# One-token attention with a gate: the queries' matrix in one load, the keys of pair 13 in one load, and the output matrix in eight pieces instead of nine

## The chip, the cores and the metric

The kernel runs on one core of one Trainium2 chip. The metric is the device time of one execution in microseconds (us). The kernel before takes 685.77 us, the median of three runs (685.71 to 686.2). All data is float32.

## The reference

The input is one token `x` of 512 numbers. It is normalised, and then goes two ways: attention of 32 heads over a cache of 8192 keys and values of 128 numbers each, and a gated product (GLU) whose result gates the attention's output.

```python
xn = layernorm(x)                                   # (1, 1, 512)
q = (xn @ wq).reshape(32 heads, 128)                # wq: 512 x 4096
p = softmax(q . k_cache * 128**-0.5)                # k_cache: 32 x 8192 x 128
o = p @ v_cache                                     # v_cache: 32 x 8192 x 128
s = o.reshape(4096) @ wo                            # wo: 4096 x 512
h = sigmoid(xn @ w_gate) * (xn @ w_up)              # 512 x 1376 each
g = silu(h @ w_down)                                # 1376 x 512
out = x + s * g
```

Keys and values are 134.2 MB each, `wq` and `wo` 8.4 MB each, the three matrices of the GLU 2.8 MB each: 293.7 MB that are each read once.

## The kernel before, in words

**Work and tiles.** Two heads make a pair, so there are 16 pairs (0 to 15). One pair's keys, or its values, are 8.4 MB: 128 partitions with 64 KB each (128 rows of 128 numbers; the heads lie on 64 partitions each). SBUF has three such slots. Slots 0 and 1 take keys: pair i lies in slot (i + 1) mod 2. Slot 2 takes values, and before them `wq` (four rows of 4096 per partition, 64 KB) and then `w_down`. Slot 0 first holds `w_gate` and `w_up`, slot 1 at the end `wo` (32 rows of 512 per partition, 64 KB).

**The loads.** All large loads are issued by SyncE (SP) on one queue, in one fixed order: `wq`, `w_gate`, `w_up`, keys 0, `w_down`, keys 1, values 0, keys 2, values 1, keys 3 and so on to values 15, then `wo`. SP waits ahead of an issue until the slot is free: keys i wait for the end of the scores of pair i-2 (`summed[i - 2]`), values i for the end of the products of pair i-1 (`valued`; for the first halves of the last two, `halved`). `w_down` waits until `wq` has been used up (`spread_all`), keys 1 until the GLU's first products are made (`rows[1]`), values 0 until the gate is made (`gated`). A load of 2 KB, `x`, comes in by ScalarE's queue.

**Ahead of the pairs.** VectorE (DVE) makes `xn`. Then `in_place` (lines 285 to 289) works on `wq` in its slot: for k = 0 to 2 it multiplies row k of each partition by its number of `xn` and adds it to row 0; the last row is added in eight parts of 512 (line 306). TensorE (PE) sums each part over the partitions with a matrix of ones, and ScalarE (ACT) copies it to the queries. The same `in_place` follows for `w_gate` and `w_up`.

**One pair.** `scores(i)` on DVE waits for the keys, multiplies them with the query (line 414) and sums them over the 128 numbers (line 415), piece by piece where the load was cut; a maximum goes by PE and DVE (`all_max`), ACT makes the powers (`powers_of`), PE multiplies them with the values (`pair`), and ACT and DVE take the result out (`parts`, `heads_out`). `K_CUTS` says where the keys' loads are cut: those of pairs 13 and 14 at three quarters, those of pair 15 at a half. `V_CUTS` cuts the last values.

**The end.** `wo` comes in pieces of whole rows r (0 to 31) that end at `W_ENDS`, so the first piece has ten rows and the last one row. Each row is 512 numbers on 128 partitions, multiplied with column r of `o_all`. Three ways share them: the rows of `W_DVE` are added up on DVE (lines 506 to 517, in order, two sums by turns); the rows of `W_PE` go through PE to `big[0]`, row number k of the list to group k mod 4 of the output's partitions; rows 28 to 31 (`direct`) go through PE to `acc`. `to_fold` adds DVE's sum and `big[0]` on DVE, `fold` adds that over the partitions into `acc` on PE. In PE's program `fold` stands between rows 30 and 31. Lines 538 and 540 gate the result and add `x`, and SP writes it out.

PE's instructions are noted down first and played later, so in the trace all of them have line 41.

Of the kernel before, what the change touches and what calls it, by code (L numbers as in the profile page):

```python
# [54 lines left out]
def kernel(  # L55
# [18 lines left out]
    NB = S // HP  # L74
    NP = H // 2
# [15 lines left out]
    FC = FL // GP  # L91
    assert F <= 3 * QT and FL % GP == 0 and 2 * KT * F <= SLOT and (FP + FC) * D <= SLOT // 2

    W_ENDS, W_FOLD = (10, 16, 20, 23, 26, 28, 30, 31, 32), 28
    W_PE = [0, 1, 10, 16, 17, 20, 21, *range(24, W_FOLD)]
    W_DVE = [r for r in range(W_FOLD) if r not in W_PE]
    V_CUTS, K_CUTS = (NB // 2, NB * 13 // 16), {NP - 3: (NB * 3 // 4,), NP - 2: (NB * 3 // 4,), NP - 1: (NB // 2,)}

    N_SEMS = 40
    DVE, ACT, SP, POOL = nc.vector, nc.scalar, nc.sync, nc.gpsimd  # L100
    PE = Later(nc.tensor)
    pe_only = OrderedEngineSet([nc.tensor.engine])
# [2 lines left out]

    sems = [nc.alloc_semaphore(f"s_{i}") for i in range(N_SEMS)]
    s_out = tc.alloc_semaphore("s_out")
# [45 lines left out]
    def semaphore(name):  # L153
        return unused.pop(0)
# [14 lines left out]
    def load(eng, name, dst, src, *after):  # L169
        wait(eng, *after)  # L170
        if name not in loads:
            loads[name] = [semaphore(f"s_{name}"), 0]
        loads[name][1] += 16
        eng.dma_start(dst, src).then_inc(loads[name][0], 16)  # L174
        return loads[name][0], loads[name][1]

    def wait(eng, *steps):
        for s in steps:
            if s is not None:
                eng.wait_ge(*s)  # L180
# [10 lines left out]
    xv = x.rearrange("a b d -> (a b d)")  # L191
    wq_t = slots[2].rearrange("p (k c) -> p k c", k=KT)
    wq_v = wq.rearrange("(p k) c -> p k c", k=KT)
    ld_wq = [load(SP, f"wq{n}", wq_t[:, n:n + 2, :], wq_v[:, n:n + 2, :]) for n in (0, 2)]
    wg_t, wu_t = (slots[0][:, n * KT * F:(n + 1) * KT * F].rearrange("p (k f) -> p k f", f=F) for n in range(2))
    ld_g = load(SP, "wg", wg_t, w_gate.rearrange("(p k) f -> p k f", k=KT))
    ld_u = load(SP, "wu", wu_t, w_up.rearrange("(p k) f -> p k f", k=KT))
# [62 lines left out]
    t = dve(DVE.reduce_sum(st[:, 0:1], x_col, axis=AX.X))  # L260
    wait(PE, t)
    t = pe(PE.matmul(pt[:, 0:1], ones, st[:, 0:1], start=True, stop=True))
    wait(DVE, t)
    t = dve(DVE.tensor_scalar(st[:, 1:2], pt[:, 0:1], 1.0 / D, None, op0=ALU.mult))
    wait(DVE, t)
    t = dve(DVE.tensor_scalar(xc, x_col, st[:, 1:2], None, op0=ALU.subtract))
    wait(DVE, t)
    t = dve(DVE.tensor_mul(sq, xc, xc))
    wait(DVE, t)
    t = dve(DVE.reduce_sum(st[:, 2:3], sq, axis=AX.X))  # L270
    wait(PE, t)
    t = pe(PE.matmul(pm[:, 0:1], ones, st[:, 2:3], start=True, stop=True))
    wait(ACT, t)
    t = act(ACT.activation(st[:, 3:4], pm[:, 0:1], AF.Sqrt, bias=eps_t, scale=1.0 / D))
    wait(DVE, t)
    t = dve(DVE.reciprocal(st[:, 4:5], st[:, 3:4]))
# [8 lines left out]
    def in_place(w, k, cols=slice(None)):  # L285
        y = w[:, 0, cols]
        if k == 0:
            return dve(DVE.tensor_scalar(y, y, xn[:, 0:1], None, op0=ALU.mult))
        return dve(DVE.scalar_tensor_tensor(y, w[:, k, cols], xn[:, k:k + 1], y, op0=ALU.mult, op1=ALU.add))  # L289
# [1 line left out]

    wait(DVE, c_xn)
    for k in range(KT - 1):
        wait(DVE, ld_wq[k // 2] if k % 2 == 0 else None, t if k else None)
        t = in_place(wq_t, k)
    wait(DVE, t)
    before_q = PE.take()
# [36 lines left out]
    for dst, src, ld in zip(sums, (wg_t, wu_t), (ld_g, ld_u)):  # L334
        wait(DVE, ld)
        for k in range(KT):
            t = in_place(src, k)
# [7 lines left out]
    for d, c in zip(sums[0], chunks):  # L345
        t = act(ACT.activation(sg[:, c], d[:, :c.stop - c.start], AF.Sigmoid))
    wait(DVE, t, rows[1])
    for d, c in zip(sums[1], chunks):
        t = dve(DVE.tensor_mul(hg[:, c], sg[:, c], d[:, :c.stop - c.start]))
# [6 lines left out]
    n = FL // NG  # L356
    for g in range(NG):
        r = slice(g * GP, (g + 1) * GP)
        h = hg[r, NG * FW + g * n:NG * FW + (g + 1) * n].rearrange("p (i c) -> p c i", c=FC)
        t = dve(DVE.transpose(hid[r, FP:, :].rearrange("p c (i m) -> p c i m", m=NG),  # L360
                              h.unsqueeze(3).to_broadcast([GP, FC, n // FC, NG])))
# [125 lines left out]
    def to_fold(after):  # L487
        wait(DVE, after, t_part)
        return dve(DVE.tensor_add(s_tmp, part[0], big[0]))
# [11 lines left out]
    def landed(eng, r, rows):  # L501
        k = rows.index(r)
        wait(eng, piece[r] if k == 0 or piece[r] != piece[rows[k - 1]] else None)

    t_parts = [placed, None]
    for k, r in enumerate(W_DVE):
        n = k % 2
# [11 lines left out]
    wait(PE, placed)  # L519
    for k, r in enumerate(W_PE):  # L520
        g = k % NG * GP
        landed(PE, r, W_PE)
        ins = PE.matmul(big[0][g:g + 1, :], o_all[:, r:r + 1], wo_t[:, r, :],
                        start=(k < NG), stop=(k + NG >= len(W_PE)))
    folded = to_fold(pe(ins))
# [12 lines left out]
    t = dve(DVE.tensor_mul(g_row, g_row, acc))  # L538
    wait(DVE, t)
    t = dve(DVE.tensor_add(g_row, g_row, x_row))  # L540
# [64 lines left out]
```

## Time and profile before

| | |
|---|---|
| three timed runs | 685.71, 685.77, 686.2 us |
| the profiled execution | 686.37 us |
| its span, from the first to the last instruction | 684.5 us |
| busy: VectorE, TensorE, ScalarE | 615.2, 218.1, 44.6 us |
| moved by the loads' queue | 293.67 MB at 429 GB/s over the span |

The profiled execution's time is 1.9 us over its span, and 0.6 us over the median of the timed runs. The trace lists for each engine its instructions with start and length in us from the start of the span, and how long the engine stood idle before one and for what. A row of the timeline may hold several like instructions (x4). SPq is SyncE's queue of issues, PEld is TensorE's loading of weights. The view by stretches gives, for chosen stretches of time, each engine's busy time and its count of instructions, the TensorE clock that was granted (1.00 is full speed), and last the loads: the time of those packets that began in the stretch as a share of it, and their bytes per second.

### The profile page before, as it was taken

The page shows a single profiled execution, that of the slowest core. Times are in us where ns is not written, and L with a number is a line of the kernel's source. Part 1 is how long each engine was busy: PE and PEld are TensorE (multiplying, and loading weights), DVE is VectorE, ACT ScalarE, POOL GpSimd, SP SyncE. Part 2 cuts the span into 40 slices and gives each one's busy share as a digit, 9 for nine tenths or more (in the row PEclk, how much of TensorE's full clock was granted, in tenths as well). Part 3 has the DMA queues.
Part 4 walks back from the last instruction along what each step waited for, and adds up shares of the span by engine and source line. Part 5 has one row for each costly group of instructions (what it writes and reads, how often), then busy time and mean ns, then how long its engine had stood idle before and what let it go on. Part 6 is the DMA issues. An engine that isn't in the chain of part 4 may idle for free. (4 is left out here: it accounts for less than half of the span.)

```text
span 684.5 us, 3423 instructions
## 1 busy us (share of the span) xinstructions
PE 218.1 (32%) x1376; PEld 61.9 (9%) x1376; DVE 615.2 (90%) x156; ACT 44.6 (7%) x142; POOL 2.6 (0%) x11
## 2 busy tenths in 40 slices
PE   0353024060513306050512406050512406060666
PEld 0120001010100101010100101010100101010110
DVE  3879999999999898998989898998989999999917
ACT  2130010000000100000000100000010101000010
POOL 0000000000000000000000000000000000000000
PEclk9996657575665757575665757575665757575886
DMA  9999999999999999999999999999999999999997
GB/s 372 433 444 463 437 429 429 429 429 429 429 429 429 429 429 429 437 463 448 429 429 429 429 429 429 429 429 429 444 467 393 472 414 414 460 419 438 429 418 320
DMA packets 7554, 293.71 MB, mean 429 GB/s; under 512 B 856, under 2 KB 864, under 8 KB 1664
## 3 DMA queue, kind: packets, MB, share of 16 engines
q1 hardware_dynamic: 7544, 293.67, 99.4%
q8 instruction: 2, 0.03, 0.0%
q10 hardware_dynamic: 8, 0.00, 0.0%
HBM read 293.67 MB, written 0.00 MB: 429 GB/s over the span
## 5 line engine op out<-in xcount | busy, mean ns | idle before, releaser
L414 DVE TENSOR_TENSOR slot<-slot,q_all 128x16384 f32<-128x16384 f32 (+3 forms) x19 | 275.9, 14522 | 21.8 <-DMA slot<-in_A_k_cache_dram 21.8
L415 DVE TENSOR_REDUCE sc<-slot 128x128 f32<-128x16384 f32 (+3 forms) x19 | 276.0, 14525 | 0.7
L41 PE MATMUL psum<-slot,zeros 128*8 128x512 f32 x1024 | 147.2, 734 | 262.9 <-PEq L41 262.9
L41 PEld LDWEIGHTS psum<-slot,zeros 128*8 128x8 f32 x1024 | 30.3, 103 | 366.3 <-issue 366.3
L41 PE MATMUL psum<-ident,mx 128*1 128x128 f32 x32 | 8.7, 371 | 105.6 <-PEq L41 105.6
L436 ACT COPY o<-psum 128x512 f32<-128x512 f32 x16 | 9.4, 586 | 408.2 <-PE psum L41 408.2
L41 PE MATMUL psum<-slot,ones 128*128 (+3 forms) x36 | 15.9, 612 | 22.9 <-PEq L41 17.5
L289 DVE SCALAR_TENSOR_TENSOR slot<-slot,xn 128x1376 f32<-128x1376 f32 (+1 forms) x8 | 18.9, 2360 | 3.0 <-DMA slot<-in_A_wq_dram 2.7
L41 PE MATMUL psum<-o,pick 128*2 128x128 f32 x128 | 16.5, 272 | 12.8 <-PEq L41 12.8
L422 DVE STREAM_TRANSPOSE psum<-psum 32x128 f32<-32x128 f32 x16 | 5.0, 310 | 11.1 <-PE psum L41 11.1
L429 ACT ACTIVATE zeros<-sc,nb 64x128 f32<-64x128 f32 x32 | 12.8, 399 | 0.9
L41 PEld LDWEIGHTS psum<-o,pick 128*2 128x2 f32 x128 | 9.9, 84 | 29.6 <-issue 27.2
L41 PE MATMUL psum<-slot,o_all 128*1 128x128 f32 (+1 forms) x54 | 10.8, 514 | 5.2 <-DMA slot<-in_A_wo_dram 5.2
L427 ACT ACTIVATE nb<-psum 128x2 f32<-128x2 f32 x16 | 2.8, 172 | 147.9 <-PE psum L41 147.9
L41 PEld LDWEIGHTS psum<-ident,mx 128*1 128x1 f32 x32 | 1.9, 80 | 109.6 <-issue 109.5
L407 DVE TENSOR_REDUCE mx<-psum 1x2 f32<-1x128 f32 x16 | 4.4, 277 | 7.8 <-PE psum L41 7.8
L41 PE MATMUL psum<-zeros,rs 128*32 128x2 f32 x32 | 3.8, 187 | 23.5 <-PEq L41 23.5
L41 PE MATMUL psum<-mx,ones 1*128 1x2 f32 x32 | 8.4, 331 | 7.4 <-PEq L41 7.4
L514 DVE SCALAR_TENSOR_TENSOR q_all<-slot,o_all,q_all 128x512 f32<-128x512 f32 x15 | 10.0, 747 | 0.0
L41 PE MATMUL psum<-slot,o 128*1 128x512 f32 x26 | 5.7, 944 | 13.0 <-DMA slot<-in_B_w_down_dram 13.0
L41 PEld LDWEIGHTS psum<-slot,ones 128*128 128x128 f32 (+1 forms) x36 | 6.3, 197 | 32.2 <-issue 24.5
L41 PEld LDWEIGHTS psum<-mx,ones 1*128 1x128 f32 x32 | 7.5, 290 | 14.3 <-issue 14.3
(54 smaller groups left out, 60.4 us busy)
## 6 DMA issues: line engine op xcount, KB each, us to landing
slot<-in_A_k_cache_dram SPq DMA_DIRECT2D x2, 6144.0 KB, 37.9
slot<-in_A_v_cache_dram SPq DMA_DIRECT2D x3, 4096.0 KB, 22.6
slot<-in_A_wq_dram SPq DMA_DIRECT2D x2, 4096.0 KB, 16.8
slot<-in_A_k_cache_dram SPq DMA_DIRECT2D x2, 4096.0 KB, 40.5
slot<-in_A_k_cache_dram SPq DMA_DIRECT2D x2, 2048.0 KB, 42.4
slot<-in_B_w_gate_dram SPq DMA_DIRECT2D x1, 2752.0 KB, 27.5
slot<-in_B_w_up_dram SPq DMA_DIRECT2D x1, 2752.0 KB, 33.5
slot<-in_B_w_down_dram SPq DMA_DIRECT2D x1, 2560.0 KB, 23.8
```

The costliest lines, as they stand in the source:

```text
L41: ins = getattr(self.engine, name)(*args, **kwargs)
L289: return dve(DVE.scalar_tensor_tensor(y, w[:, k, cols], xn[:, k:k + 1], y, op0=ALU.mult, op1=ALU.add))
L407: DVE.reduce_max(mx[:1, 1:3], pt[0:1, :].rearrange("o (e p) -> o e p", e=2), axis=AX.X).then_inc(reduced, 1)
L414: wait(DVE, dve(DVE.tensor_mul(k[:, j, :], k[:, j, :], qb[:, i:i + 1, :].to_broadcast([P, n, Dh]))))
L415: summed[i] = dve(DVE.reduce_sum(sc[i % 2][:, j], k[:, j, :], axis=AX.X))
L422: turned_out[i] = dve(DVE.transpose(o, pn.rearrange("e (a r) -> e a r", r=WR)))
L427: wait(ACT, act(ACT.mul(nb, pm[:, :2], -SCALE)))
L429: ACT.activation(weights[h, :, e * HT:(e + 1) * HT], sc[i % 2][h].rearrange("p (g b) -> p g b", b=HT), AF.Exp, bias=nb[h, e:e + 1], scale= ...
L436: ACT.copy(o1, po).then_inc(copied, 1)
L514: ins = DVE.scalar_tensor_tensor(part[n], wo_t[:, r, :], col, part[n], op0=ALU.mult, op1=ALU.add)
```

## The change

`wq` is loaded by one DMA instead of two, each with two of the four rows of a partition; `in_place` waits for the whole. The keys of pair 13 come by one DMA and go through one multiplication and one sum; those of pairs 14 and 15 stay cut. `wo` comes in eight pieces instead of nine, with 10, 7, 5, 4, 2, 2, 1 and 1 rows instead of 10, 6, 4, 3, 3, 2, 2, 1 and 1. PE has rows 0, 1, 15, 16, 20, 21, 22, 24 to 27 instead of 0, 1, 10, 16, 17, 20, 21, 24 to 27; eleven rows stay with PE, 17 with DVE, and rows 28 to 31 are treated as before. Three semaphores fewer are used.

```diff
-    W_ENDS, W_FOLD = (10, 16, 20, 23, 26, 28, 30, 31, 32), 28
-    W_PE = [0, 1, 10, 16, 17, 20, 21, *range(24, W_FOLD)]
+    W_ENDS, W_FOLD = (10, 17, 22, 26, 28, 30, 31, 32), 28
+    W_PE = [0, 1, 15, 16, 20, 21, 22, *range(24, W_FOLD)]
     W_DVE = [r for r in range(W_FOLD) if r not in W_PE]
-    V_CUTS, K_CUTS = (NB // 2, NB * 13 // 16), {NP - 3: (NB * 3 // 4,), NP - 2: (NB * 3 // 4,), NP - 1: (NB // 2,)}
-    N_SEMS = 40
+    V_CUTS, K_CUTS = (NB // 2, NB * 13 // 16), {NP - 2: (NB * 3 // 4,), NP - 1: (NB // 2,)}
+    N_SEMS = 37
...
-    ld_wq = [load(SP, f"wq{n}", wq_t[:, n:n + 2, :], wq_v[:, n:n + 2, :]) for n in (0, 2)]
+    ld_wq = load(SP, "wq", wq_t, wq_v)
...
     for k in range(KT - 1):
-        wait(DVE, ld_wq[k // 2] if k % 2 == 0 else None, t if k else None)
+        wait(DVE, t if k else ld_wq)
         t = in_place(wq_t, k)
```

## The prediction

> **What bounds the kernel now.** First the page: the busy shares, the loads in 40 slices, the loads' queue.
>
> ```profile
> span 684.5 us, 3423 instructions
> PE 218.1 (32%) x1376; PEld 61.9 (9%) x1376; DVE 615.2 (90%) x156; ACT 44.6 (7%) x142; POOL 2.6 (0%) x11
> DMA  9999999999999999999999999999999999999997
> q1 hardware_dynamic: 7544, 293.67, 99.4%
> ```
>
> The loads' queue fills its 16 engines for 99.4% of the span; VectorE (DVE) is busy for 90%, but no slice shows the loads waiting for it. So the time is a stream of 293.67 MB, what lies ahead of it, and what lies behind its last byte. An edit that leaves the bytes alone acts in three ways only: it changes what a transfer costs beside its bytes, it makes the stream run dry, or it changes the work behind the last landing. Next the timeline of the start, for the stream's cover.
>
> ```profile
> 8.30 0.40 DVE L259 STREAM_TRANSPOSE g_row<-x_row 128x128 f32<-128x128 f32 x1 [6.92 <-DMA x_row<-in_A_x_dram]
> 11.55 0.23 DVE L278 TENSOR_SCALAR xn<-xc,st 128x4 f32<-128x4 f32 x1
> 13.14 2.35 DVE L288 TENSOR_SCALAR slot<-slot,xn 128x4096 f32<-128x4096 f32 x1 [1.36 <-DMA slot<-in_A_wq_dram]
> 15.53 4.48 DVE L289 SCALAR_TENSOR_TENSOR slot<-slot,xn 128x4096 f32<-128x4096 f32 x1
> 22.74 4.49 DVE L289 SCALAR_TENSOR_TENSOR slot<-slot,xn 128x4096 f32<-128x4096 f32 x1 [2.73 <-DMA slot<-in_A_wq_dram]
> 48.80 0.33 SPq L174 DMA_DIRECT2D slot<-in_A_k_cache_dram  x1
> 61.74 5.70 PE L41 MATMUL psum<-slot,o 128*1 128x512 f32 x26 [12.98 <-DMA slot<-in_B_w_down_dram]
> 68.58 0.33 SPq L224 DMA_DIRECT2D slot<-in_A_v_cache_dram  x1
> 90.36 0.33 SPq L174 DMA_DIRECT2D slot<-in_A_k_cache_dram  x1
> 100.41 8.59 PE L41 MATMUL psum<-slot,zeros 128*8 128x512 f32 x64 [5.10 <-PEq L41]
> 109.07 0.33 SPq L224 DMA_DIRECT2D slot<-in_A_v_cache_dram  x1
> ```
>
> The four issues of SyncE are keys 1, values 0, keys 2 and values 1. TensorE (PE) begins at 100.41, when values 0 have landed: keys 2 were issued 10 us before that. When the stream takes up the next transfer is seen in the view by stretches; the last number is the rate of the packets that began there.
>
> ```profile
> 0.00:1.80 1.80, 0.00 (x0) 0.00 (x0) 0.17 (x1) 0.00 (x0) 0.74 (x8) 1.00 0.00 0
> 1.80:2.40 0.60, 0.00 (x0) 0.00 (x0) 0.00 (x0) 0.00 (x0) 0.43 (x3) 1.00 3.19 874
> 97.60:99.30 1.70, 0.00 (x0) 0.00 (x0) 1.70 (x1) 0.00 (x0) 0.00 (x0) 0.50 0.00 0
> 99.30:100.00 0.70, 0.00 (x0) 0.00 (x0) 0.70 (x1) 0.00 (x0) 0.00 (x0) 0.50 3.47 1498
> ```
>
> Even with no load ahead of it, the first packets began after 1.80, so an issue becomes packets within about 2 us of the start of the program; the first packets of keys 2 began after 99.30, when values 0 let the engines go.
>
> **Part 1, `wq` whole.** DVE's first operation on `wq` starts not at 13.14 but when the whole has landed, about 22.74, where the third operation starts now. The two that were done in the meantime, from 13.14 to 15.53 + 4.48 = 20.01, now lie behind that: everything that follows on DVE moves by 6.9 us. Queued behind this wait are the GLU's products and all scores. Who pays? Not DVE, which later waits for keys anyway (a row of pair 14 below). SyncE's issues move with it, on one queue: `w_down` (until `wq` is used up), keys 1, values 0, keys 2. Keys 1: 48.80 becomes 55.7, before the end of `w_down` at 61.7. Values 0: 68.58 becomes at most 75.5; keys 1 take 19.3 us (half of a pair, next part) after `w_down`, until 81. Keys 2: 90.36 becomes 97.2; they must be packets at 99.3. With the 2 us at most from issue to packet that is 99.2, just in time; the true delay is shorter, since the first issue itself came after the program's own start. Values 1: 109.07 becomes at most 115.9; keys 2 land at 100.4 + 19.3 = 119.7. After that the margin grows, since a pair's stream is longer than its DVE work. So the cost is nothing, hidden by the transfer that runs meanwhile, with 0.1 to 1.1 us left at the tightest place; without that cover each us more would cost one.
>
> One detail: the small load of `x` waits behind packets of `wq`, and these double, from 32 to 64 KB. It waits 6.92 us now; at twice that, `x` would be there at 8.3 + 6.9 = 15.2, and `xn` 3.5 us later (8.30 to 11.78) at 18.7: before 22.74. No cost.
>
> **Part 2, keys of pair 13 whole.** The timeline of pair 13, with DVE, PE and SyncE:
>
> ```profile
> 526.01 9.12 PE L41 MATMUL psum<-slot,zeros 128*8 128x512 f32 x64 [19.98 <-PEq L41]
> 542.36 12.94 DVE L414 TENSOR_TENSOR slot<-slot,q_all 128x12288 f32<-128x12288 f32 x1
> 564.70 8.55 PE L41 MATMUL psum<-slot,zeros 128*8 128x512 f32 x64 [19.93 <-PEq L41]
> 572.65 4.42 DVE L415 TENSOR_REDUCE sc<-slot 128x32 f32<-128x4096 f32 x1
> 577.10 0.81 SPq L174 DMA_DIRECT2D slot<-in_A_k_cache_dram  x2
> 579.07 12.96 DVE L414 TENSOR_TENSOR slot<-slot,q_all 128x12288 f32<-128x12288 f32 x1 [0.84 <-DMA slot<-in_A_k_cache_dram]
> ```
>
> PE starts at 526.01 and 564.70 as values 11 and 12 land: 38.7 us for keys and values, 19.35 each. So keys 13 land whole at 545.35. Now DVE starts on three quarters at 542.36 and ends at 577.07; then it starts at 545.4 and needs the same 34.7 us, or a little less: 580.1 at most, 3.0 late. Behind that wait stands only DVE's own queue, and SyncE's issue of keys 15, 577.10 to 580.1, which has values 13 (issued before, landing 38.6 after 564.70, at 603.3) ahead of it: hidden by over 20 us. Pair 14 now waits 0.84 us for its keys; that goes, and 2.2 us of lateness stay. With keys 15 there in good time, DVE keeps it to the end. What is late next is the last pair's product:
>
> ```profile
> 653.25 7.79 PE L41 MATMUL psum<-slot,zeros 128*8 128x512 f32 x52
> 661.45 1.89 PE L41 MATMUL psum<-slot,zeros 128*8 128x512 f32 x12 [0.42 <-PEq L41]
> 665.76 0.21 DVE L471 STREAM_TRANSPOSE o_all<-psum 32x32 f32<-32x32 f32 x1
> ```
>
> PE starts at 655.4 instead of 653.25, does not stop for the last piece of values any more (0.42 idle), and ends up to 1.8 late; then the last heads are placed at 666.0 + 1.8 = 667.8, where `wo`'s first rows are used from 667.41 on. That is 0.4 late on a sum of DVE that has 0.65 us to spare (the row at 679.61 below). No cost.
>
> **Part 3, the end.** The rows of `wo`:
>
> ```profile
> 667.41 0.88 DVE L512 TENSOR_SCALAR q_all<-slot,o_all 128x512 f32<-128x512 f32 x2 [1.44 <-DMA slot<-in_A_wo_dram]
> 668.21 10.02 DVE L514 SCALAR_TENSOR_TENSOR q_all<-slot,o_all,q_all 128x512 f32<-128x512 f32 x15
> 671.13 0.09 PEld L41 LDWEIGHTS psum<-slot,o_all 128*1 128x1 f32 x2 [3.52 <-DMA slot<-in_A_wo_dram]
> 677.24 0.09 PEld L41 LDWEIGHTS psum<-slot,o_all 128*1 128x1 f32 x4 [1.76 <-DMA slot<-in_A_wo_dram]
> 678.53 1.03 PE L41 MATMUL psum<-slot,o_all 128*1 128x512 f32 x4 [0.27 <-DMA slot<-in_A_wo_dram]
> 679.61 0.69 DVE L489 TENSOR_TENSOR q_all<-q_all,psum 128x512 f32<-128x512 f32 x1 [0.65 <-PE psum L41]
> 680.61 0.40 PE L41 MATMUL psum<-q_all,ones 128*1 128x128 f32 x8
> 681.02 0.40 PE L41 MATMUL psum<-slot,o_all 128*1 128x128 f32 x8
> ```
>
> What a transfer costs beside its bytes: from 667.41 to 671.13 six rows came in one piece, 3.72 us; from 677.24 to 681.02 six rows came in four pieces, 3.78 us. Three pieces more cost 0.06 us, 0.02 each. Three transfers fewer (one of `wq`, one of keys 13, one of `wo`) gain 0.06 us; from nothing to 0.15 I take 0.1. [...]
>
> Rows come at (681.02 - 667.41) / 22 = 0.62 us each, so the new pieces are there at 671.7 (rows 10 to 16), 674.8 (17 to 21), 677.3 (22 to 25), 678.55 (26, 27), and the last three as now. DVE has 17 rows as before, two from 667.41 and 15 at 0.67: row 10 at 672.2, row 17 at 675.6, row 23 at 677.6, each behind its landing, the end as now at 678.2.
>
> PE is another matter. It gets rows 15 and 16 at 671.7, rows 20 and 21 at 674.8, and rows 22, 24 and 25 at 677.3, where it now has rows 24 and 25 alone. Rows in different groups run side by side: 22, 24 and 25 are in groups 2, 3 and 0, so three take as long as two. How long depends on the clock:
>
> ```profile
> 670.17:673.58 3.41, 1.87 (x2) 0.09 (x2) 3.41 (x7) 0.00 (x0) 0.00 (x0) 0.50 0.97 410
> 673.58:676.99 3.41, 3.40 (x8) 0.18 (x8) 3.41 (x7) 0.00 (x0) 0.00 (x0) 0.50 1.00 419
> ```
>
> One batch of rows takes PE 1.87 us at the clock of 0.50 (first stretch), 1.03 us at full clock (rows 26 and 27 at 678.53). The clock rose only after a stretch that PE had filled, 3.40 of 3.41 us; the stretch before, filled to 1.87, brought nothing. After the change PE has 1.87 us from 674.8 and then nothing until 677.3: in that same stretch it fills 55%, and the clock would stay at 0.50 until about 680.4. Then rows 22, 24, 25 take until 679.0 (two passes of about 0.85 us), rows 26 and 27 until 680.9, and DVE's `to_fold` starts at 680.9, not 679.61. `fold` stands ahead of row 31 in PE's queue, and now ends at 681.01, just as that row lands at 681.02. So at most 1.3 us, at full clock for `fold` 1.0 us, come behind the last landing. Where the stretches lie elsewhere against the program, one that begins at 674.8 to 676 is filled to 80% or more, the clock rises at 678.2 to 679.4, and the loss is 0 to 0.4 us. I take 0.3 us, with 0 and 1.3 as ends, nearer to the lower, since half of the places for the stretch lose under that.
>
> The Trainium skill, "TensorE: Matmul & The Clock Gate", section "Part 1: The HAM clock gate", has TensorE at half rate until it has been busy through a window of about 3.4 us, and says that the window runs free of the kernel's start. By a strict reading the clock cannot rise before rows 26 and 27 are done, the loss is the 1.0 us above, and the sum 0.9 slower; the two stretches agree with it, but a stretch filled to 80% is in neither.
>
> **Sum.** -0.1 for the transfers, 0 for `wq`, 0 for pair 13, +0.3 for the end: +0.2 on the span of 684.5. The profiled execution took 686.37, 0.6 over the median of the runs; I put the difference on the median, 685.77 + 0.2 = 686.0.
>
> **The rivals.**
> *The stream runs dry ahead of keys 2* (slower). Its place is 99.3. It decides as soon as keys 2 are issued later than about 98.3, a shift of 8 us instead of 6.9; each us more costs one. It would happen if `x` came only behind the whole of `wq`: then `xn` is there at 22.7 + 3.5 = 26.2, the shift is 10.3, keys 2 are issued at 100.7 and are packets 1 to 2 us later, at about 101.7: 2.4 us lost, 688.4. For it: the margin is small. Against: `x` now comes at 8.30, well before even the first half of `wq`. 8%.
> *The clock stays low at the end*: +1.0 - 0.1, 686.7. For it: the two stretches. Against: the stretches need not lie where they did. 25%.
> *Every transfer has its own fixed cost on the stream.* If the up to 2 us from issue to packets, seen at the start, were paid at each transfer, three fewer would save 6 us: 679.8. Against: six rows in four pieces. 2%. [...]
>
> **How the numbers follow.** My forecast, 685.6 to 686.5, has 61%; with the three rivals that is 96%, and 2% each are for something unseen on either side. A measurement of this kernel can tell about 0.2%, 1.4 us, from no change. Forecast and low clock lie within that (86%); the dry stream and one unseen part are slower (10%); the fixed cost and the other are faster (4%). The range, 685.3 to 687.2, holds the forecast, the low clock and the loss of 1.3 us with some spread of the runs (0.5 us now).
>
> **What would show it.** Right: the first operation on `wq` starts near 22.7 and keys 2 are issued near 97.2, with packets beginning in every stretch around 99.3 as before; keys 13 wait about 3 us, and values 13 land where they do now less 0.1; row 31 lands 0.1 earlier, and `to_fold` tells by its start between 679.5 and 680.9 which clock PE had. Wrong: PE's start on values 0 and all later landings move by a us or more (the stream ran dry), `wo`'s first rows are used clearly after 667.9 (pair 13's lateness reached the end), or the landings come several us earlier (a fixed cost).

## The result, and the profile after

| | median of 12 runs, us | lowest to highest |
|---|---|---|
| before | 686.33 | 685.71 to 686.92 |
| after | 688.27 | 686.53 to 689.65 |

The ratio is 1.0025, with a 95% interval of 1.0016 to 1.0033: the kernel is 1.9 us slower at the medians. 686.0 was forecast, and the range ended at 687.2. The execution that was profiled took 689.65 us, the slowest of the twelve; so its trace shows the losses larger than the usual run has them, 3.3 us over the span of before in all.

The page of after, to be read beside the first lines shown of before:

```profile
span 687.8 us, 3416 instructions
DMA  8999989999999999999999999999999999999996
q1 hardware_dynamic: 7112, 293.67, 98.9%
```

Fewer packets (7112, not 7544), the same bytes, yet 98.9% in place of 99.4%: the engines of the loads stood still somewhere. The row of slices has an 8 in the first slice and in the sixth (86 to 103 us), where before has 9. The timeline of the start, DVE, TensorE (PE), GpSimd (POOL) and SyncE's issues (SPq):

```profile
10.63 0.40 DVE L259 STREAM_TRANSPOSE g_row<-x_row 128x128 f32<-128x128 f32 x1 [9.24 <-DMA x_row<-in_A_x_dram]
22.83 2.35 DVE L288 TENSOR_SCALAR slot<-slot,xn 128x4096 f32<-128x4096 f32 x1 [8.71 <-DMA slot<-in_A_wq_dram]
34.26 5.39 DVE L306 SCALAR_TENSOR_TENSOR slot<-slot,xn 128x512 f32<-128x512 f32 x8
45.60 2.23 DVE L288 TENSOR_SCALAR slot<-slot,xn 128x1376 f32<-128x1376 f32 x1
45.71 1.38 POOL L322 MEMSET slot<- 128x1536 f32 x1 [43.36 <-PE psum L41]
52.94 4.95 PE L41 MATMUL psum<-slot,ones 128*128 128x512 f32 x6 [3.82 <-DVE slot L289]
99.49 0.33 SPq L174 DMA_DIRECT2D slot<-in_A_k_cache_dram  x1
140.79 8.62 PE L41 MATMUL psum<-slot,zeros 128*8 128x512 f32 x64 [1.88 <-PEq L41]
```

The same places in before:

```profile
37.36 1.38 POOL L322 MEMSET slot<- 128x1536 f32 x1 [35.02 <-PE psum L41]
38.60 0.94 DVE L288 TENSOR_SCALAR slot<-slot,xn 128x1376 f32<-128x1376 f32 x1
44.65 4.12 PE L41 MATMUL psum<-slot,ones 128*128 128x512 f32 x6 [3.46 <-DVE slot L289]
139.37 9.58 PE L41 MATMUL psum<-slot,zeros 128*8 128x512 f32 x64 [9.59 <-PEq L41]
```

Keys 2 were issued at 99.49, not at the forecast 97.2: the shift against 90.36 is 9.1 us, not 6.9. The first multiplication of `w_up` (L288) took 2.23 us in place of 0.94, beside GpSimd's fill of a part of the slot (L322), which in before was over when that operation began; that is 1.3. PE's products behind it took 4.95 in place of 4.12, 0.8 more; the clock granted to them was 0.50, and 0.61 on average in before. The stretches of after where keys 2 are taken up:

```profile
99.40:100.40 1.00, 0.48 (x2) 0.11 (x2) 0.34 (x2) 0.00 (x0) 0.00 (x0) 0.50 0.01 0
100.40:101.30 0.90, 0.44 (x3) 0.36 (x2) 0.75 (x2) 0.00 (x0) 0.00 (x0) 0.50 3.46 1165
```

In before, packets of keys 2 began in 99.30 to 100.00 at 1498 GB/s. Here none begin until 100.4: the stream is dry for about a microsecond. All sixteen engines then begin by 101.30 (1165 GB/s for 0.90 us are 16 packets of 64 KB), and these packets take longer: the share in the row, 3.46, times 0.90 us is 3.1 us for each of 16, and 3.47 times 0.70 is 2.4 in before. Values 1 are used at 140.79, 1.4 later than the 139.37 of before. Then the end:

```profile
565.82 1.04 PE L41 MATMUL psum<-slot,zeros 128*8 128x512 f32 x4 [20.09 <-PEq L41]
604.54 1.90 PE L41 MATMUL psum<-slot,zeros 128*8 128x512 f32 x8 [19.93 <-PEq L41]
639.90 10.76 SPq L224 DMA_DIRECT2D slot<-in_A_v_cache_dram  x3
669.97 0.88 DVE L512 TENSOR_SCALAR q_all<-slot,o_all 128x512 f32<-128x512 f32 x2 [1.43 <-DMA slot<-in_A_wo_dram]
683.37 0.69 DVE L489 TENSOR_TENSOR q_all<-q_all,psum 128x512 f32<-128x512 f32 x1 [1.87 <-PE psum L41]
```

Lateness against before, step by step: 1.1 us where values 12 are used (564.70 before), 2.6 at `wo`'s first rows (667.41), 3.8 at `to_fold` (679.61). So there are three losses: one near 100 us, one between 604 and 670, one after 670. `to_fold` waited 1.87 us for PE, whose clock was low:

```profile
676.47:679.88 3.41, 1.99 (x7) 0.19 (x10) 3.41 (x6) 0.00 (x0) 0.00 (x0) 0.50 1.00 415
679.88:683.29 3.41, 3.41 (x22) 1.00 (x20) 1.59 (x3) 0.00 (x0) 0.00 (x0) 0.50 0.57 222
```

### The profile page after: what moved, and what is told of

The parts are those of the page before. It is cut to its first block, busy times and chain, and to the rows that moved or that the text cites. A ratio compares the mean times of both kernels' runs of the same rounds, so it can differ in the third digit from the quotient of the medians.

```text
span 687.8 us, 3416 instructions
## 1 busy us (share of the span) xinstructions
PE 225.0 (33%) x1376; PEld 64.2 (9%) x1376; DVE 616.0 (90%) x154; ACT 44.6 (6%) x142; POOL 2.6 (0%) x11
## 3 DMA queue, kind: packets, MB, share of 16 engines
q1 hardware_dynamic: 7112, 293.67, 98.9%
## 5 line engine op out<-in xcount | busy, mean ns | idle before, releaser
L41 PE MATMUL psum<-slot,zeros 128*8 128x512 f32 x1024 | 152.7, 758 | 210.8 <-PEq L41 210.8
L41 PE MATMUL psum<-slot,ones 128*128 (+3 forms) x36 | 18.0, 677 | 27.6 <-PEq L41 22.2
L289 DVE SCALAR_TENSOR_TENSOR slot<-slot,xn 128x1376 f32<-128x1376 f32 (+1 forms) x8 | 18.9, 2360 | 0.3
L288 DVE TENSOR_SCALAR slot<-slot,xn 128x1376 f32<-128x1376 f32 (+1 forms) x3 | 5.5, 1837 | 8.8 <-DMA slot<-in_A_wq_dram 8.7
```

The costliest lines, as they stand in the source:

```text
L41: ins = getattr(self.engine, name)(*args, **kwargs)
```

## The experiments

Each is timed against the kernel before on the same chip; the ratio stands with its 95% interval.

**Each part of the change alone.** First `wq` whole:

```diff
-    ld_wq = [load(SP, f"wq{n}", wq_t[:, n:n + 2, :], wq_v[:, n:n + 2, :]) for n in (0, 2)]
+    ld_wq = load(SP, "wq", wq_t, wq_v)
```

> The kernel before with wq in one load, and nothing else of the change. Theory A (the stream runs dry ahead of keys 2, because everything on DVE starts 6.9 us later, and GpSimd's fill of w_down's rest then falls on DVE's multiplication of w_up): keys 2 are issued at 98 to 99.5 instead of 90.4, no packets begin for up to 0.5 us after values 0, all later landings are 0 to 1.4 us late; +0.3 to +1.4 us on the kernel before, most of the 1.9 us of the whole change. Theory B (the new rows of wo keep TensorE at half clock at the end): +0, since the end is as before. Theory C (pair 13's lateness reaches the end): +0.

Then the keys of pair 13 whole:

```diff
-    K_CUTS = {NP - 3: (NB * 3 // 4,), NP - 2: (NB * 3 // 4,), NP - 1: (NB // 2,)}
+    K_CUTS = {NP - 2: (NB * 3 // 4,), NP - 1: (NB // 2,)}
```

> The kernel before with the keys of pair 13 in one load, and nothing else of the change. Theory C: the last heads are placed later than wo's first rows land, +0.5 us or more. Theories A and B: +0 (within 0.3 us); DVE waits 3 us for keys 13, and the heads are placed by 667.9.

Then the pieces of `wo` and their deal:

```diff
-    W_ENDS, W_FOLD = (10, 16, 20, 23, 26, 28, 30, 31, 32), 28
+    W_ENDS, W_FOLD = (10, 17, 22, 26, 28, 30, 31, 32), 28
-    W_PE = [0, 1, 10, 16, 17, 20, 21, *range(24, W_FOLD)]
+    W_PE = [0, 1, 15, 16, 20, 21, 22, *range(24, W_FOLD)]
```

> The kernel before with wo's eight pieces and the rows dealt out anew, and nothing else of the change. Theory B: rows 22, 24 and 25 come at half clock, to_fold starts up to 1.3 us later; +0.3 to +1.0 us in the median and a wider spread of the runs than the kernel before. Theories A and C: +0.

| part alone | median, us | before, us | ratio |
|---|---|---|---|
| `wq` whole | 687.89 | 686.37 | 1.0017 [1.0008, 1.0025] |
| keys 13 whole | 686.34 | 686.37 | 0.9998 [0.9989, 1.0006] |
| `wo` in eight pieces | 687.04 | 686.37 | 1.0006 [0.9997, 1.0015] |

The differences add up to 2.2 us, against 1.9 for the whole. `wq` is the main part, and its trace holds the surprise, timeline and stretches:

```profile
97.30 0.33 SPq L174 DMA_DIRECT2D slot<-in_A_k_cache_dram  x1
140.65 9.32 PE L41 MATMUL psum<-slot,zeros 128*8 128x512 f32 x64 [3.92 <-PEq L41]
```
```profile
99.30:100.10 0.80, 0.04 (x1) 0.00 (x0) 0.80 (x1) 0.71 (x2) 0.00 (x0) 0.50 2.88 1229
100.10:100.40 0.30, 0.00 (x0) 0.00 (x0) 0.30 (x1) 0.30 (x1) 0.00 (x0) 0.50 0.00 0
100.40:100.60 0.20, 0.00 (x0) 0.00 (x0) 0.20 (x1) 0.20 (x1) 0.00 (x0) 0.50 1.08 328
```

In this run the issue stands where the prediction had it, at 97.30, and still values 1 are used at 140.65, 1.3 late. 1229 GB/s for 0.8 us are 983 KB, 15 packets of 64 KB; 328 GB/s for 0.2 us are one more. So 15 engines took the new transfer up at 99.3 to 100.1, as in before, and the sixteenth only after 100.4, 3.1 us behind the issue; its packet took 1.08 x 0.20 x 16 = 3.5 us, not 2.4. DVE and PE wait for the whole transfer, so for its last engine, and the lag stays: values 13 are still used 1.1 late (604.46 against 603.33). The expectation had the issue at 98 to 99.5, because the fill would fall on `w_up` here too; in this trace it cost 0.2 us (L288 took 1.14), and the loss came without it.

For `wo` alone, timeline and stretch:

```profile
680.78 0.69 DVE L489 TENSOR_TENSOR q_all<-q_all,psum 128x512 f32<-128x512 f32 x1 [1.86 <-PE psum L41]
```
```profile
677.20:680.50 3.30, 3.30 (x18) 0.79 (x20) 1.69 (x3) 0.00 (x0) 0.00 (x0) 0.50 0.97 385
```

The clock stays at 0.50 to 680.5, and `to_fold` starts at 680.78, 1.2 after that of before; the median is 0.7 us higher, in an interval that still holds no difference.

**GpSimd's fill out of the way.** The fill and the small load behind it move from ahead of the GLU's loop to behind its first multiplication of `w_up`.

```diff
-    wait(POOL, spread_all)
-    c_rest = pool(POOL.memset(wd_rest, 0.0))
...
+            if rows and k == 0:
+                wait(POOL, spread_all, t)
+                c_rest = pool(POOL.memset(wd_rest, 0.0))
```

> The whole change, but GpSimd's fill of w_down's rest (1.4 us) waits until DVE has done its first operation on w_up, so that it falls on another DVE operation. Theory A with this cause: w_up's first operation takes 0.94 us again, not 2.23; keys 2 are issued 1.3 us earlier, at about 98.2 in a run like the profiled one, and the stream no longer runs dry: 0.5 to 1.3 us faster than the whole change, +0.6 to +1.4 on the kernel before. If the collision is not what makes it late: +1.9 as with the whole change.

```profile
45.70 0.94 DVE L288 TENSOR_SCALAR slot<-slot,xn 128x1376 f32<-128x1376 f32 x1
46.76 1.39 POOL L337 MEMSET slot<- 128x1536 f32 x1 [44.41 <-DVE slot L288]
```

The 2.23 us are 0.94 again, with the fill beside L289 instead: the collision is shown. Keys 2 are issued at 97.62. The median is 686.99, ratio 1.0015 [1.0001, 1.0028], an interval too wide to tell it from the change. Of the twelve runs eight lie between 685.96 and 687.15 and four between 689.48 and 690.20; the trace is of one of the four. An issue at 97.62 is still inside the 3.1 us found above, and values 1 are used at 140.45, 1.1 late.

**Keys 2 late, with nothing else changed.** On the kernel before, a second, unused sum ahead of the scores of pair 0 makes them late: over 52 columns in the first run, 30 in the second.

```diff
+        if i == 0:
+            wait(DVE, ld_k[0][0][1])
+            wait(DVE, dve(DVE.reduce_sum(sc[1][:, :52], k[:, :52, :], axis=AX.X)))
```

> The kernel before with one more sum on DVE, 7.0 us, ahead of pair 0's scores (its result is not used), so that keys 2 are issued at about 97.4 instead of 90.4 and everything ahead of it stays. Theory A (a late issue of keys 2 alone costs the time, as soon as it comes within about 2.5 us of the end of values 0, since one of the 16 DMA engines then takes the new transfer up late): keys 2 land about 1.3 us late, +1.0 to +1.6 us, like wq in one load. If the stream must be dry on all engines to cost anything: keys 2 come in time and it is +0. If it is something else that wq in one load changes at the start: +0.

> The same with 4.0 us: keys 2 are issued at about 94.5, 5 us ahead of the end of values 0. Theory A: +0 (within 0.3 us), all engines take the transfer up without a gap. If each us on DVE costs something: about 4/7 of the run with 7 us.

These two do not measure the stream alone: 690.56, ratio 1.0060 [1.0044, 1.0077], and 688.61, ratio 1.0035 [1.0022, 1.0048]. The first one's trace has keys 2 issued at 97.17, values 1 used at 140.88, 1.5 late, and the result written at 684.24. The second one's trace has keys 2 issued at 96.13, values 1 used at 139.03, and the result written when it was in before (682.12):

```profile
682.08 0.64 SPq L571 DMA_DIRECT2D out_dram<-g_row  x1
```
```profile
q14 instruction: 3, 0.02, 0.0%
```

Its span is nevertheless 686.9: the 2.3 us lie behind the result, in the program's close. The first one, too, ends 4.6 us after that write, 684.24 to 688.8, and before 2.4. The queue "q14 instruction" is in these two traces and not in that of before. DVE's drain at the close (line 110) comes 3.8 us later than in before, though the result was written on time (the first line is of before, the other two are of this run):

```profile
L110 DVEq DRAIN  x1: 110/110/110, 682.0 to 682.0; - x1
L110 DVEq DRAIN  x1: 117/117/117, 685.8 to 685.8; - x1
683.70:683.90 0.20, 0.00 (x0) 0.00 (x0) 0.00 (x0) 0.00 (x0) 0.00 (x0) 1.00 0.17 41
```

Between, at 683.70 to 683.90, a packet of 8 KB begins (41 GB/s for 0.20 us), long after the loads; before has none at 683.70 to 684.10. I read this as DVE's program, two instructions longer, still being fetched; the packet's queue and its time fit, but that it holds DVE's program is not shown. So the same two sums were run again on the kernel with keys 13 whole, whose DVE program is two operations shorter and whose time was that of before.

> The run with 7.0 us more on DVE once more, on the kernel with the keys of pair 13 in one load (which alone cost nothing), so that DVE's program is not longer than before: in the two runs before, DVE's last instructions came 2.3 us late, because its longer program was still being fetched at the end, and that is no part of the question. Theory A: keys 2 are issued at 97 to 98.5, one or more of the 16 engines take them up late, +1.0 to +2.2 us, and the span ends 2.4 us after the write of the result is issued, as before. If the 4.2 us of the first such run were all from the fetch or from the longer DVE work: +0.

> The same with 4.0 us: keys 2 are issued at 94.4 to 96, at least 3.4 us ahead of the end of values 0. Theory A: +0, within 0.4 us. If each us counts: about +1.

```profile
97.62 0.33 SPq L174 DMA_DIRECT2D slot<-in_A_k_cache_dram  x1
141.10 8.45 PE L41 MATMUL psum<-slot,zeros 128*8 128x512 f32 x64 [4.05 <-PEq L41]
```
```profile
96.52 0.33 SPq L174 DMA_DIRECT2D slot<-in_A_k_cache_dram  x1
139.95 8.81 PE L41 MATMUL psum<-slot,zeros 128*8 128x512 f32 x64 [4.01 <-PEq L41]
```

At 97.62 values 1 are 1.7 late and the time is 687.85, ratio 1.0020 [1.0010, 1.0029], with `wq` as it was: a late issue alone makes the loss. At 96.52, 1.1 earlier, values 1 are 0.6 late and the time is 686.43, ratio 1.0006 [0.9997, 1.0015]. Both traces are of the slowest run of their kernel. In the one with 7 us twelve engines began by 100.10, two more by 100.40 and two after that: it need not be one engine. In the one with 4 us all sixteen began in time, as 1311 GB/s for 0.80 us are 16 packets:

```profile
99.30:100.10 0.80, 0.00 (x0) 0.00 (x0) 0.80 (x1) 0.79 (x2) 0.00 (x0) 0.50 3.18 1311
```

They took 3.18 x 0.80 = 2.54 us on average, not 2.4, so some took longer; this is the only sign of the 0.6 in these rows.

**The whole change, with the margin given back.** Pair 0's scores in two halves, and keys 2 in two loads, so that the first is issued as soon as the first half is summed.

```diff
+            if i == 2:
+                load_keys(i, V_HALVES[:1], first_sum[0])
+                load_keys(i, V_HALVES[1:], summed[0])
```

> The whole change, with pair 0's scores made in two halves and the keys of pair 2 loaded in two halves, the first issued when DVE has done with the first half of pair 0 (17 us earlier). wq stays in one load and DVE stays as late. Theory A: no gap after values 0, landings as in the kernel before; 1.2 to 1.9 us faster than the whole change, +0.2 to +0.7 on the kernel before (the end's rows stay). If the loss of wq in one load lies elsewhere: +1.7 as the whole change.

```profile
82.03 17.65 SPq L174 DMA_DIRECT2D slot<-in_A_k_cache_dram  x2
139.26 8.90 PE L41 MATMUL psum<-slot,zeros 128*8 128x512 f32 x64 [0.49 <-PEq L41]
602.95 3.60 PE L41 MATMUL psum<-slot,zeros 128*8 128x512 f32 x16 [20.05 <-PEq L41]
638.62 9.06 SPq L224 DMA_DIRECT2D slot<-in_A_v_cache_dram  x3
668.17 0.88 DVE L518 TENSOR_SCALAR q_all<-slot,o_all 128x512 f32<-128x512 f32 x2 [1.40 <-DMA slot<-in_A_wo_dram]
```

The first part is issued at 82.03, and the loss at values 1 is gone (139.26). The time is 687.08, ratio 1.0011 [1.0002, 1.0020]: better by 1.2 us at the medians than the change (the intervals overlap a little), and not whole. In this trace the rest has one place: behind `wo`'s first rows nothing is lost (`to_fold` at 680.36, 12.19 later; in before 12.20). From values 13 to `wo`'s first rows this run takes 668.17 - 602.95 = 65.22 us, where before takes 667.41 - 603.33 = 64.08 and after 669.97 - 604.54 = 65.43. The issue of values 15 stands 638.62 - 602.95 = 35.67 us behind values 13 here and 35.36 in after; in before it is 34.5:

```profile
603.33 3.60 PE L41 MATMUL psum<-slot,zeros 128*8 128x512 f32 x16 [22.76 <-PEq L41]
637.85 10.37 SPq L224 DMA_DIRECT2D slot<-in_A_v_cache_dram  x3
```

So over a microsecond is lost again where an issue comes a microsecond nearer to the end of the stream ahead of it: the second loss. What brings it nearer is PE, whose products of pair 14 stand ahead of that issue and took 6.24 us in after and 5.42 in before, by the clock granted to them (first before, then after):

```profile
634.00:638.00 4.00, 3.78 (x28) 0.70 (x20) 4.00 (x1) 0.00 (x0) 0.00 (x0) 0.75 1.18 508
634.00:638.00 4.00, 4.00 (x24) 0.83 (x20) 4.00 (x2) 0.00 (x0) 0.00 (x0) 0.50 1.10 475
```

But the distance alone does not decide. The run with 4 us (first form) has that issue 638.64 - 603.18 = 35.46 us behind values 13, and uses `wo`'s first rows 667.37 - 603.18 = 64.19 behind them, so it loses nothing there:

```profile
638.64 9.06 SPq L224 DMA_DIRECT2D slot<-in_A_v_cache_dram  x3
667.37 0.88 DVE L515 TENSOR_SCALAR q_all<-slot,o_all 128x512 f32<-128x512 f32 x2 [1.43 <-DMA slot<-in_A_wo_dram]
```

How near is too near is therefore not known for this place.

**The clock at the end.** Products that nobody uses fill PE's waits ahead of and between the rows of `wo`, on the kernel before and on the kernel with the new deal of `wo` alone.

```diff
+    def filler(n):
+        for _ in range(n):
+            PE.matmul(big[1][0:1, :], ones[:, 0:1], slots[0][:, :QT], start=True, stop=True)
+    filler(2)
     wait(PE, placed)
```

> The kernel before with six matrix products more on TensorE in the waits of the end (two ahead of wo's first rows, two after rows 0 and 1, one after row 10, one after rows 16 and 17), into a bank that nobody reads. Theory B (TensorE's clock falls in the waits of the end, and what it costs depends on where its window lies in a run): the clock stays at 1.00 through the end, to_fold starts as soon as rows 26 and 27 have come; -0.1 to -0.6 us in the median, and a narrower spread of runs than the kernel before. If the clock does not matter at the end: +0, or up to +0.5 where an extra product is in the way.

> The kernel before with wo's eight pieces and the new deal, and seven products more on TensorE in the waits of the end (two ahead of wo's first rows, two after rows 0 and 1, two after rows 15 and 16, one after rows 20 and 21). Theory B (the new deal costs because the clock stays at 0.50): to_fold starts at 679.5 to 679.8 and not 680.8, 0.4 to 0.7 us faster than the new deal without them, -0.1 to +0.1 on the kernel before. If the new deal costs for another reason: +0.4 as without them.

On before: 686.27, ratio 1.0001 [0.9992, 1.0010], with runs from 685.80 to 687.22: neither the gain nor the narrower spread that theory B expected. In its trace `to_fold` comes 12.18 us behind `wo`'s first rows, and 12.20 in before, so there was nothing to gain there. On the new deal: 686.33, ratio 1.0001 [0.9992, 1.0010], where it had 1.0006 [0.9997, 1.0015] without them; the two intervals overlap, and it is the trace that tells them apart.

```profile
679.63 0.69 DVE L489 TENSOR_TENSOR q_all<-q_all,psum 128x512 f32<-128x512 f32 x1 [0.56 <-PE psum L41]
```
```profile
677.20:680.50 3.30, 2.69 (x28) 0.51 (x30) 2.52 (x4) 0.00 (x0) 0.00 (x0) 1.00 1.01 403
```

At a clock of 1.00 the new deal's `to_fold` starts at 679.63, as that of before: the 1.2 us of the other trace were the clock, and the deal itself costs nothing.

**The second place.** The first part of the last two pairs' values is cut smaller, so that it can be issued earlier; once on the kernel with keys 13 whole, once on the change.

```diff
-    V_CUTS = (NB // 2, NB * 13 // 16)
+    V_CUTS = (NB * 3 // 8, NB * 13 // 16)
...
-            for v, cut in ((i - 1, V_HALVES), (i, V_THREE)):
+            for v, cut in ((i - 1, V_THREE), (i, V_THREE)):
```

> A candidate: the kernel before with the keys of pair 13 in one load, and the values of pairs 14 and 15 both in three pieces (48, 56 and 24 of 128 rows per partition instead of halves, and 64, 40 and 24). The issue of values 15 then comes 6 us or more, not 3, ahead of the end of the transfer before it. Theory A, applied to the second place where an issue comes close to the end of the transfer ahead of it: no engine lags there any more; -0.1 to -0.4 us in the median and fewer runs over 686.6. If that place costs the kernel before nothing: +0.

> The whole change with the values of pairs 14 and 15 in three pieces each (48, 56, 24), so that values 15 are issued 6 us or more ahead of the end of the transfer before, and nothing else: keys 2 still come late, and the rows of wo stay with the new deal. If an engine that lags since keys 2 is what makes the second place at values 15 cost up to 2 us more, that second loss goes: runs over 688.5 vanish, the median is 0.5 to 1.0 us under that of the whole change, about +1.0 on the kernel before. If the slowest runs come from keys 2 and the end alone: +1.7 as the whole change.

On keys 13 whole: 686.35, ratio 0.9999 [0.9990, 1.0008], no gain. On the change: 687.76, ratio 1.0016 [1.0007, 1.0025], half a microsecond below the change at the medians, with intervals that overlap widely, and three of eleven runs are still over 688.5, which the expectation had ruled out. In its trace the issue of values 15 stands 636.08 - 604.84 = 31.24 us behind values 13, and `wo`'s first rows are used at 669.29, 64.45 behind them, in place of 65.43 in after: most of the second loss is gone there. Its size in the usual run is not settled.

**All three repairs on the change**: keys 2 in halves, values 14 in three, the fillers.

> The whole change with all three repairs at once: keys 2 in two pieces with the first issued early (pair 0's scores in two parts), the values of pairs 14 and 15 in three pieces, seven products more on TensorE in the waits of the end. If late issues at two places and the clock at the end are all that the change costs: -0.2 to +0.2 us on the kernel before, with its narrow spread. If a fourth cost is left: more than +0.4.

```profile
139.15 8.90 PE L41 MATMUL psum<-slot,zeros 128*8 128x512 f32 x64 [0.48 <-PEq L41]
667.40 0.88 DVE L518 TENSOR_SCALAR q_all<-slot,o_all 128x512 f32<-128x512 f32 x2 [1.02 <-DMA slot<-in_A_wo_dram]
679.51 0.69 DVE L495 TENSOR_TENSOR q_all<-q_all,psum 128x512 f32<-128x512 f32 x1 [0.56 <-PE psum L41]
```

686.40 against 686.52, ratio 0.9997 [0.9988, 1.0006], apart from the 1.0016 to 1.0033 of the change. The three steps are back where they were in before (139.37, 667.41, 679.61): within that interval the three losses are the whole of what the change cost. No version was measurably faster than before.

## Why the prediction was wrong, step by step

**Part 1: the step that failed.** The prediction took "the 2 us at most from issue to packet" from the start of the program, and so "the cost is nothing, hidden by the transfer that runs meanwhile". The mechanism (a shift of DVE that carries keys 2 to the end of their cover) was right, and so was the tightest place. Two sizes were off, and the term that they gave, 0 for `wq`, measured +1.5 us alone.

The bound itself: at the start of the program all sixteen engines had begun by 2.40 us (874 GB/s for 0.6 us, in the prediction's stretches, are 16 packets of 32 KB). It holds again in after, where the stream had run dry: all began by 101.30, 1.8 us behind the issue at 99.49. It does not hold while the transfer ahead still runs: with the issue at 97.30, as forecast, one engine began 3.1 us behind it. Nor did the prediction count that first packets can take longer, 3.5 us in place of 2.4 on that engine. The lead that costs nothing is longer than 2 us; the issue of keys 2 against values 1:

| run | keys 2 issued, us | values 1 used, us | later than before, us |
|---|---|---|---|
| before | 90.36 | 139.37 | |
| 4 us late (first form) | 96.13 | 139.03 | none |
| 4 us late (second form) | 96.52 | 139.95 | 0.6 |
| 7 us late (first form) | 97.17 | 140.88 | 1.5 |
| `wq` whole | 97.30 | 140.65 | 1.3 |
| 7 us late (second form) | 97.62 | 141.10 | 1.7 |
| the change, fill later | 97.62 | 140.45 | 1.1 |
| the change, values 14 in three | 99.26 | 140.60 | 1.2 |
| the change | 99.49 | 140.79 | 1.4 |

With values 0 letting the first engines go near 99.4, 3.3 us of lead lost nothing, 2.9 us lost 0.6, 2.2 and less 1.1 to 1.7. It is a step, not the rival's "each us more costs one": between 97.17 and 99.49 the price does not grow, as one late engine is enough to make the whole transfer late. These are single executions: values 1 are used between 138.92 and 139.39 in the six traces with keys 2 issued at 90 to 92, and the runs of the change differ by 3 us. Why some engines come late, or have longer first packets, is open.

The Trainium skill, "DMA: Bandwidth & Descriptors", section "Latency and other measured facts", gives about 0.6 us to the first byte of a DMA that SyncE issues. With the stream dry, in after, the trace has the first packets 0.9 us behind the start of the issue and 0.6 behind its end (99.49 and 0.33 long, packets from 100.40). As a lead that suffices it does not serve: 2.1 us did not.

The shift: the 6.9 us counted what the waiting operations move, 7.0 measured (L306 began at 34.26, and at 27.26 in before). They did not count what the moved work then meets: 1.3 us from GpSimd's fill, which did not move with it by the same amount, and 0.8 from PE at a clock of 0.50. So of the "0.1 to 1.1 us left" nothing was left at 99.49. In the traces that added little: `wq` alone, issued at 97.30, paid as much.

The Trainium skill, "SBUF — State Buffer", section "Who interferes with whom", says that GpSimd and VectorE share a pair of ports as a lock for a whole instruction, that a `tensor_scalar` can be of the kind that takes it, and that one with two inputs in SBUF meets only GpSimd's reads. The traces agree in the main: L288 went from 0.94 to 2.23 beside the fill, and L289, with two inputs, lay beside the same fill in before and in the run with the fill moved, at no cost. In all five traces in which the fill meets L288 (the change, `wq` whole, keys 2 in halves, values 14 in three, all three repairs), L288 ends 0.7 us after the fill does (47.83 and 47.09 in after): it waits for the fill's end. By that page, who issues first wins; here the one that starts first by the trace, L288 by 0.11 us, is the longer one.

`x` landed for 10.63, within the 15.2 allowed: right, so the rival's cause did not occur; the rival's event, a dry stream ahead of keys 2, did, by other causes. It had 8%. Its time, 688.4, lies 0.1 from the measured 688.27 by luck: it had 2.4 us lost at keys 2 alone.

**Part 2: right at its own place, and blind behind it.** Keys 13 whole alone cost nothing (0.9998). DVE waited 3.04 us for them, as forecast, in after:

```profile
546.44 17.23 DVE L414 TENSOR_TENSOR slot<-slot,q_all 128x16384 f32<-128x16384 f32 x1 [3.04 <-DMA slot<-in_A_k_cache_dram]
```

What the prediction followed were the heads, not the next transfer: it did not ask how far ahead of the stream values 15 are issued, the same bound as in part 1, in a second place. Keys 13 are not what brings that issue nearer: with them whole alone it stands 637.43 - 603.21 = 34.22 us behind values 13, in before 34.5. It is PE's clock in pair 14, which no part of the prediction looked at.

**Part 3: right mechanism, a term that was taken too small.** The clock stayed at 0.50 as the rival "the clock stays low" had it; `to_fold` of the new deal alone began at 680.78, inside the forecast 679.5 to 680.9. Of the ends 0 and 1.3 the prediction took 0.3; the part alone is 0.7 over before at the median. Three transfers fewer, -0.1, is too small to be seen in any median; no saving of a fixed 2 us per transfer showed, so that rival fell.

Of the sum, then: for `wq` +1.5 at the median in place of 0, for the end +0.7 in place of +0.3, and nothing for keys 13; 2.2 together, 1.9 measured, and +0.2 forecast. Between 686.0 and 688.27 lie another 0.6 us: the forecast stood on 685.77, the median of three runs, and twelve gave 686.33.

## What to carry to other kernels

When a kernel is bound by one stream of loads, the margin to watch is the lead of each issue over the end of the transfer ahead of it, in every place of the queue; at keys 2 here 3.3 us lost nothing and 2.9 already 0.6, and the slowest of the sixteen engines decides. When work is moved, list what runs on the other engines at its new time (a fill by GpSimd, a clock at half) before the shift is called a number.

## What the runs showed of the hardware that was not expected

- An engine that takes a transfer up late stays late: 1.3 us at 140 us are still 1.1 us at values 13 in the run with `wq` alone (604.46 against 603.33).
- Two more instructions on DVE made the program's close 2.3 us longer with the result written on time (682.08 against 682.12); with the same sum and DVE's program as long as before, the close was 2.4 to 2.6 us again (685.39 to 687.8, 683.47 to 686.1).
- A VectorE multiplication that meets a GpSimd fill of 1.38 us waits for it: in five traces it ends 0.7 us after the fill (47.83 and 47.09 in after).
- PE need not be busy without a gap to keep its clock: the fillers kept it busy for 2.69 of 3.30 us, and it stayed at 1.00.
